# Where the transform matrices are made in the parameter stage, and what the first table round carries beside it

## The chip, the cores and the metric

The kernel runs on one core of a Trainium2 chip. The metric is the device time of one execution in microseconds (us); several executions of each kernel are timed and the median is taken. One more execution is recorded by the hardware profiler, and all durations below come from that one. Engines are named as in the profile: PE (matrix multiply), PEld (its weight loads), DVE (vector engine), ACT (scalar engine), POOL (GpSimd) and SP (the engine that issues most of the DMAs).

## What is computed

Two independent results are laid side by side. A is a recurrent attention block (2048 tokens in 64 segments of 32, a memory of 8 tokens carried from segment to segment). B is a long convolution whose 2048-tap filter is first built from complex parameters, then applied in the frequency domain. The change lies in front of both, in the stages that prepare B's filter and the part of A that does not depend on the carried memory.

```python
# B: filter, then convolution by FFT
dt = exp(log_dt)[:, None]
logdA = dt * (A_re + 1j * A_im);  dB = dt * (B_re + 1j * B_im)
P = exp(logdA[:, :, None] * l[None, None, :])          # D x N x L
K = einsum('dn,dnl,dn->dl', C_re + 1j * C_im, P, dB).real
y = irfft(rfft(pad(u)) * rfft(pad(K)))[:L] + u * Dskip
# A, for each segment s (mem is carried on):
h = concat([mem, x_s]);  q, k, v = h @ Wq, h @ Wk, h @ Wv
o = softmax(mask(q k^T * scale)) v @ Wo;  mem = o[:, :8];  out_s = o[:, 8:]
```

## The kernel before

`part_b` does B and, beside it, the projections of A for the 8 rows of every segment that never see the carried memory. Its first half has two stages that matter here.

**The parameter stage** (lines 679 to 856, inside one `with` block). Vector and scalar instructions turn the parameters into four tables x1 to x4 of 128 x 1024 numbers. Each is split by `put3` into three bf16 pieces (`hi`, `mid`, `lo`) that are stored to the DRAM tensor `PB`. Three other things are made meanwhile, as generators that `run` steps in turn:

- `modulus` and `angle`, which compute x4 and x3; x3 comes out last;
- `ahead.transposes` (lines 92 to 113): 16 blocks of x are loaded by POOL (`xb`), transposed by PE into `pt_x` (`ppt`, four PSUM banks) and copied by ACT into `xst` and `xTl`. The projections read the whole of `xTl`;
- `matrices` (lines 738 to 756): ten rounds that make the cosine and sine matrices `MF` of the transform. A full round is, on DVE, one absolute value (L744), one magic-number subtraction (L748) and two multiplies (L753), and on ACT a cosine (L745), a sine (L749) and a rounding (L755). Two rounds are made at the very start, three during the first `run`, the rest during the second.

An engine executes its instructions in the order in which they were written, so these pieces stand interleaved on DVE and ACT.

**The table stage** (loop over `f` from -1 to 16, lines 1159 to 1189). Sixteen rounds `r` of one table each go through the word list `ORDER`. A word with a prime belongs to round f-1, one without to round f. `X_t`, `X_p` are PE matmuls into `ptt` and `pa`; `k` (L1094) and `n` (L1100) reduce phases; `E` (L1088) takes exponentials on ACT; `S`, `C` take sines and cosines on ACT (L1105, L1114), with `b` (L1111) and `w` (L1118) on DVE between them; `gi`, `gr` (L1062, L1063) are the products on DVE; `K` (L949) and `x` (L957) form filter values, which are stored to `Kd`. E and S/C need different ACT tables, so each round has two ACT table loads (L1088, L1105).

The side jobs stand in the same list:

- `P0` to `P5` are six projection jobs. A job is one half of a weight slice: eight matmuls of 512 columns (L167) or sixteen of 256 (L154) into a PSUM tile of the pool `ps_k` (tag "s", four buffers), evicted later by a word `p0` to `p5` on DVE or ACT. There are 48 slices, so 96 jobs. The slice loads (`wsl`, L125, four buffers) are issued by SP three slices ahead. When the last job of a tensor is evicted, the stores of its results (`PKd`, or the eight row copies `VXd<-PVd`, L133) are put on a list `late`, from which each later eviction takes two.
- `U0` to `U3` are four jobs of `side` (L905): the forward transform of u with `MF`. They run in groups of four: results 0 and 1 are copied to `ua` on ACT, results 2 and 3 are subtracted and added on DVE into `us` (L916, L917), and after the fourth POOL combines them (`ux`, L921, L922, L924) and stores them to `Ud`. The first U job issues the loads `u_h` (L873) of u.
- `M` transposes one MF matrix (L884), evicted by `m` to `ms` and stored to `MId`.

Four P jobs are done before the loop. In the loop, side jobs run in every round from f = 0 on, primed words too; `evict_of` fixes which engine evicts. At f = 15 what is pending is flushed, `ahead.late` is emptied, and SP and POOL load the filter `KT` from `Kd` (L996). At f = 16 PE starts with `spectrum(0)` (L1050) and DVE with `negate` (KN, L1033). After the loop, the frequency-domain product (`pointwise`, L1224 to L1235 on DVE) begins.

Of the kernel before, what the change touches and what calls it, by code (L numbers as in the profile page):

```python
# [16 lines left out]
PSUM = bass.MemoryType.PSUM  # L17
# [628 lines left out]
def part_b(ctx, tc, u, A_re, A_im, B_re, B_im, C_re, C_im, log_dt, Dskip, out_b, ahead, copies, residents, first_state):  # L646
# [6 lines left out]
    v, sc, gp, pe, sy = nc.vector, nc.scalar, nc.gpsimd, nc.tensor, nc.sync  # L653
# [15 lines left out]
    MF = ahead.pool.tile([128, 4, 16, 2, 128], BF16, name="MF", tag="MF")  # L669

    ctx1 = ctx.enter_context(ExitStack())
    tabs = ctx1.enter_context(tc.tile_pool(name="b_tab", bufs=1))
    RE = tabs.tile([128, 8, NE], BF16, name="RE")
    RT = tabs.tile([128, 8, NT], BF16, name="RT")
# [5 lines left out]
    with tc.tile_pool(name="b_par", bufs=1) as par, tc.tile_pool(name="b_parh", bufs=2) as parh, tc.tile_pool(name="b_mg", bufs=2) as mg, \  # L680
# [11 lines left out]
        def f32(name):  # L692
            return par.tile(sh, F32, name=name)

        def put3(x, q, row):
            hi = parh.tile(sh, BF16, name="hi", tag="hi")
            sc.copy(out=hi[:], in_=x[:])
            sy.dma_start(out=PB[q][row].rearrange("t p n -> p t n"), in_=hi[:])
            yield
            v.tensor_tensor(out=x[:], in0=x[:], in1=hi[:], op=ALU.subtract)  # L700
            mid = parh.tile(sh, BF16, name="mid", tag="mid")
            sc.copy(out=mid[:], in_=x[:])
            sy.dma_start(out=PB[q][row + 1].rearrange("t p n -> p t n"), in_=mid[:])
            yield
            lo = parh.tile(sh, BF16, name="lo", tag="lo")
            v.tensor_tensor(out=lo[:], in0=x[:], in1=mid[:], op=ALU.subtract)
            sy.dma_start(out=PB[q][row + 2].rearrange("t p n -> p t n"), in_=lo[:])
            yield

        def run(*gens):  # L710
            gens = list(gens)
            while gens:
                for g in list(gens):
                    if next(g, g) is g:
                        gens.remove(g)
# [11 lines left out]
        def some(g, n):  # L727
            for _ in range(n):
                next(g, None)
                yield  # L730
# [7 lines left out]
        def matrices():  # L738

            tms, kMs = {}, {}  # L740
            for c in range(0, 20, 2):
                if 4 <= c:
                    tm = tms.pop(c - 4)
                    v.tensor_scalar(out=tm[:].bitcast(I32), in0=tm[:].bitcast(I32), scalar1=0x7FFFFFFF, scalar2=None, op0=ALU.bitwise_and)  # L744
                    sc.activation(out=sines(c - 4, 0), in_=columns(tm), func=ACT.Sin, scale=-TWO_PI, bias=hp[:])  # L745
                if 2 <= c < 18:
                    tm = tms[c - 2]
                    v.scalar_tensor_tensor(out=tm[:], in0=kMs.pop(c - 2)[:], scalar=MAGIC, in1=tm[:], op0=ALU.subtract, op1=ALU.subtract)  # L748
                    sc.activation(out=sines(c - 2, 1), in_=columns(tm), func=ACT.Sin, scale=-TWO_PI)  # L749
                if c < 16:  # L750
                    tms[c] = mg.tile([128, 2, 512], F32, name="tm", tag="tm", bufs=4)
                    for i in range(2):
                        v.tensor_scalar(out=tms[c][:, i], in0=colk[:], scalar1=rowl[:, c + i:c + i + 1], scalar2=None, op0=ALU.mult)  # L753
                    kMs[c] = mg.tile([128, 2, 512], F32, name="mkM", tag="mkM")
                    sc.activation(out=kMs[c][:], in_=tms[c][:], func=ACT.Identity, bias=magic[:])  # L755
                yield

        dt_b = dtb[:].unsqueeze(2).to_broadcast(sh)
        mats = matrices()
# [38 lines left out]
        x1, x2, x3, x4, x5, Wr, Wi = (f32(n_) for n_ in ("x1", "x2", "x3", "x4", "x5", "Wr", "Wi"))  # L798
# [14 lines left out]
        def modulus():  # L813

            sc.activation(out=y1[:], in_=Wi[:], func=ACT.Square)
            sc.activation(out=y2[:], in_=Wr[:], func=ACT.Square)
            yield
            v.tensor_tensor(out=x4[:], in0=y1[:], in1=y2[:], op=ALU.add)
            v.tensor_scalar(out=x4[:], in0=x4[:], scalar1=1.0e-37, scalar2=None, op0=ALU.max)
            sc.activation(out=x4[:], in_=x4[:], func=ACT.Ln)  # L820

            sc.activation(out=y1[:], in_=Wr[:], func=ACT.Abs)
            sc.activation(out=y2[:], in_=Wi[:], func=ACT.Abs)
            yield
            v.tensor_scalar(out=x4[:], in0=x4[:], scalar1=0.5, scalar2=None, op0=ALU.mult)
            yield

        def angle():

            v.tensor_tensor(out=x5[:], in0=y1[:], in1=y2[:], op=ALU.max)  # L830
            v.tensor_scalar(out=x5[:], in0=x5[:], scalar1=1.0e-37, scalar2=None, op0=ALU.max)
            v.reciprocal(out=x5[:], in_=x5[:])
            v.tensor_tensor(out=x3[:], in0=y1[:], in1=y2[:], op=ALU.min)
            v.tensor_tensor(out=x3[:], in0=x3[:], in1=x5[:], op=ALU.mult)
            sc.activation(out=x3[:], in_=x3[:], func=ACT.Arctan)
            yield
            v.tensor_scalar(out=x3[:], in0=x3[:], scalar1=float(1.0 / TWO_PI), scalar2=None, op0=ALU.mult)
            v.tensor_tensor(out=y1[:], in0=y2[:], in1=y1[:], op=ALU.is_gt)
            v.tensor_scalar(out=y2[:], in0=Wr[:], scalar1=0.0, scalar2=None, op0=ALU.is_lt)
            v.tensor_scalar(out=Wi[:], in0=Wi[:], scalar1=0.0, scalar2=None, op0=ALU.is_lt)  # L840
            yield
            for msk, top in ((y1, 0.25), (y2, 0.5)):
                v.tensor_scalar(out=x5[:], in0=x3[:], scalar1=-2.0, scalar2=top, op0=ALU.mult, op1=ALU.add)
                v.tensor_tensor(out=x5[:], in0=x5[:], in1=msk[:], op=ALU.mult)
                v.tensor_tensor(out=x3[:], in0=x3[:], in1=x5[:], op=ALU.add)
                yield
            v.tensor_scalar(out=Wi[:], in0=Wi[:], scalar1=-2.0, scalar2=1.0, op0=ALU.mult, op1=ALU.add)
            v.tensor_tensor(out=x3[:], in0=x3[:], in1=Wi[:], op=ALU.mult)
            yield
            yield from put3(x3, 1, 3)  # L850

        xs = ahead.transposes(prx, ppt, ident)
        pro = ahead.projections()
        next(pro)
        run(modulus(), put3(x2, 1, 0), put3(x1, 0, 0), some(xs, 9), some(mats, 3))
        run(xs, angle(), xs, put3(x4, 0, 3), xs, mats)


    tmp = ctx1.enter_context(tc.tile_pool(name="b_tmp", bufs=2))
# [2 lines left out]
    ctx_p = ctx.enter_context(ExitStack())  # L862
    ps_t = ctx_p.enter_context(tc.tile_pool(name="b_pst", bufs=2, space=PSUM))
    ps_e = ctx_p.enter_context(tc.tile_pool(name="b_pse", bufs=1, space=PSUM))
    ps_k = ctx1.enter_context(tc.tile_pool(name="b_psk", bufs=4, space=PSUM))

    u_r = u.rearrange("(c p r) d -> r p c d", p=128, r=4)

# [1 line left out]
    def load_uq(dq):  # L870
# [1 line left out]
        for r in range(4):  # L872
            sy.dma_start(out=t_[:, 4 * r:4 * r + 4, :], in_=u_r[r][:, :, DQ * dq:DQ * dq + DQ])  # L873
        return t_[:].rearrange("p c (t s e) -> p c s t e", t=4, e=8)

    def take(shape, dtype, name):
        return ps_k.tile(shape, dtype, name=name, tag="s")

    def matrices_back():
        for c in range(16):  # L880
# [269 lines left out]
    for eng, names in ((sc.copy, ON_ACT), (v.tensor_copy, ON_DVE)):  # L1150
        for nm, kind, slot in names:
            evict_of[nm] = (kind, slot, eng)
    evict = pro.send((take, tabs))
    for i in range(3):
        evict_next = next(pro)
        evict((sc.copy, v.tensor_copy)[i % 2])
        evict = evict_next
    evict(v.tensor_copy)
    for f in range(-1, 17):
        if f == 15:  # L1160
            for kind, slot in sorted(k for k in pending if k[0] == "P"):
                run_evict(kind, slot, v.tensor_copy)
            while ahead.late:
                ahead.late.pop(0)()
            ks = [load_k(0, DH, (sy, gp), ahead.pool.tile([128, 16, DH], BF16, name="KT", tag="kst"))]
        if f == 16:
            spectra = [load_u(0), load_u(1)]
        for word in ORDER:
            nm, r = word.rstrip("'"), f - word.endswith("'")
            if f == 16 and word == ORDER[0]:  # L1170
                s0 = ps_e.tile([128, 2, 512], F32, name="pa", tag="pa")
                s1 = [ps_t.tile([128, 512], F32, name="ptt", tag="ptt") for _ in range(2)]
                first = [[s0[:, half, :].rearrange("p (c d) -> p c d", c=2) for half in range(2)],
                         [t_[:].rearrange("p (c d) -> p c d", c=2) for t_ in s1]]
                negate(ks[0], v)
                spectrum(0, first)
            if nm in evict_of:
                run_evict(*evict_of[nm])
            elif nm[0] in side_ops:
                if f >= 0:  # L1180
                    run_side(nm[0], int(nm[1:] or 0))
            elif nm[0] == "X":
                e = int(nm[1])
                if 0 <= r <= 15 - (e == 0) or (r == -1 and e == 0):
                    table_ops[nm[2]](r, e)
            elif 0 <= r <= 15:
                table_ops[nm[:-1]](r, int(nm[-1]))
# [329 lines left out]
```

## Time and profile before

| | us |
|---|---|
| median of 3 runs | 2136.48 (2134.81 to 2144.58) |
| the profiled execution, device time | 2141.16 |
| the profiled execution, span of the trace | 2139.4 |

| busy over the span | share | instructions |
|---|---|---|
| PE | 88% | 33734 |
| DVE | 67% | 3353 |
| ACT | 49% | 1915 |
| POOL | 20% | 780 |

In the trace the parameter stage lies from 0 to about 83 us, the table stage from there to about 478 us, the frequency-domain part to about 728 us, and the attention segments behind it to the end. The page divides the span into 40 slices, so two slices cover the parameter stage and seven the table stage. A line of a timeline, as shown below, reads: start, duration, engine, source line, operation, output<-input with sizes, how many were merged, and in brackets how long the engine sat idle before it and what ended that. A line of stretches reads: the stretch, its length, and for each engine the busy time with the number of instructions, then the granted PE clock, the DMA share and GB/s.

### The profile page before, as it was taken

The page shows a single profiled execution, that of the slowest core. Times are in us where ns is not written, and L with a number is a line of the kernel's source. Part 1 is how long each engine was busy: PE and PEld are TensorE (multiplying, and loading weights), DVE is VectorE, ACT ScalarE, POOL GpSimd, SP SyncE. Part 2 cuts the span into 40 slices and gives each one's busy share as a digit, 9 for nine tenths or more (in the row PEclk, how much of TensorE's full clock was granted, in tenths as well). Part 3 has the DMA queues.
Part 4 walks back from the last instruction along what each step waited for, and adds up shares of the span by engine and source line. Part 5 has one row for each costly group of instructions (what it writes and reads, how often), then busy time and mean ns, then how long its engine had stood idle before and what let it go on. Part 6 is the DMA issues. An engine that isn't in the chain of part 4 may idle for free. (4 is left out here: it accounts for less than half of the span.)

```text
span 2139.4 us, 78633 instructions
## 1 busy us (share of the span) xinstructions
PE 1885.6 (88%) x33734; PEld 1183.7 (55%) x33734; DVE 1442.0 (67%) x3353; ACT 1045.2 (49%) x1915; POOL 435.8 (20%) x780
## 2 busy tenths in 40 slices
PE   1589999977999779999999999999998998999999
PEld 1365656656888535555555555555554555555554
DVE  8589999989999246566566665666655565666650
ACT  6699999971333324444444444444434343444430
POOL 2145445452111101111111111111111111111121
PEclk9999999989999889999999999999999999999999
DMA  6767886556745899999999999999998999999991
GB/s 162 191 198 229 241 226 176 163 174 204 242 134 175 302 350 328 324 324 338 319 337 333 325 322 324 328 335 338 324 321 302 320 323 317 308 334 334 327 335 57
DMA packets 344019, 590.78 MB, mean 276 GB/s; under 512 B 108537, under 2 KB 220185, under 8 KB 341621
## 3 DMA queue, kind: packets, MB, share of 16 engines
q1 hardware_dynamic: 297016, 528.00, 74.1%
q0 software_dynamic: 10544, 33.69, 4.6%
q10 hardware_dynamic: 36108, 24.07, 3.7%
q8 instruction: 264, 4.33, 0.8%
q14 instruction: 87, 0.70, 0.1%
HBM read 530.86 MB, written 65.26 MB: 279 GB/s over the span
## 5 line engine op out<-in xcount | busy, mean ns | idle before, releaser
L365 PEld LDWEIGHTS <-a_hT 128*32 128x32 bf16 x12352 | 337.5, 96 | 326.5 <-issue 79.6
L371 ACT CAST arena<-acc 128x512 bf16<-128x512 f32 x384 | 224.9, 586 | 421.2 <-PE acc L365 274.6
L365 PE MATMUL acc<-W,a_hT 128*32 128x512 bf16 x4864 | 376.1, 383 | 0.0
L474 PEld LDWEIGHTS <-arena 128*32 128x32 bf16 x8256 | 211.2, 97 | 110.8 <-issue 54.1
L365 PE MATMUL acc<-wst,a_hT 128*32 128x512 bf16 x2304 | 234.3, 385 | 40.2 <-DMA wst<-WD_v 28.9
L292 DVE TENSOR_SCALAR arena<-keep 128x256 int32<-128x256 int32 (+1 forms) x512 | 175.8, 395 | 35.6 <-PE acc L365 31.8
L379 POOL COPY arena<-arena 128x128 bf16<-128x128 bf16 x128 | 37.3, 292 | 720.9 <-PE tr L376 236.5
L474 PE MATMUL pp<-W_o,arena 128*32 128x256 bf16 x4608 | 171.9, 275 | 10.8 <-DMA W_o<-in_A_Wo_dram 6.7
L365 PE MATMUL acc<-MF,a_hT 128*32 128x512 bf16 x2048 | 158.7, 381 | 0.0
L414 DVE TENSOR_REDUCE a_mx<-sc 128x4 f32<-128x160 f32 (+1 forms) x192 | 73.0, 380 | 124.7 <-ACT sc L410 124.7
L167 PE MATMUL pro<-xTl,wsl 128*128 128x512 bf16 x512 | 119.8, 385 | 5.2 <-ACT xTl L111 5.2
L489 DVE COPY arena<-tr 128x512 bf16<-128x512 bf16 x64 | 27.2, 424 | 141.9 <-PE tr L376 96.7
L1050 PEld LDWEIGHTS <-MF 128*128 128x128 bf16 x1024 | 102.6, 101 | 29.9 <-issue 8.6
L410 ACT ACTIVATE sc<-sc 128x160 f32<-128x160 f32 (+1 forms) x192 | 64.2, 334 | 105.0 <-DVE sc L407 100.7
L437 POOL TENSOR_TENSOR arena<-arena,a_BD 128x128 bf16<-128x128 bf16 x128 | 68.5, 535 | 229.8 <-DVE arena L424 212.8
L460 ACT CAST arena<-pv 128x512 bf16<-128x512 f32 x128 | 75.1, 587 | 80.3 <-PE pp L444 59.0
L406 DVE TENSOR_REDUCE a_mx<-sc 128x4 f32<-128x160 f32 (+1 forms) x192 | 71.8, 374 | 59.2 <-PE sc L394 58.1
L567 ACT CAST arena<-pp 128x128 bf16<-128x128 f32 x128 | 27.8, 269 | 163.6 <-PE pp L474 163.6
L1050 PE MATMUL hps<-KT,MF 128*128 128x256 bf16 x720 | 94.1, 283 | 14.7 <-DVE x L1225 11.6
L1282 PE MATMUL yp<-Bt,MI 128*128 128x256 bf16 x680 | 102.8, 273 | 0.8 <-ACT yb L1298 0.8
L1088 ACT ACTIVATE E<-pa 128x648 bf16<-128x648 f32 x128 | 91.3, 713 | 17.9 <-PE pa L1080 14.2
L376 PEld LDWEIGHTS <-arena 128*128 128x128 bf16 x1024 | 57.9, 98 | 75.1 <-issue 37.4
(316 smaller groups left out, 4100.9 us busy)
## 6 DMA issues: line engine op xcount, KB each, us to landing
wst<-WD_v SPq DMA_DIRECT2D x256, 512.0 KB
wst<-WD_k SPq DMA_DIRECT2D x192, 512.0 KB
wst<-WD_o SPq DMA_DIRECT2D x192, 512.0 KB
wst<-WD_q SPq DMA_DIRECT2D x128, 512.0 KB
Ud<-ux POOLq DMA_DIRECT2D x16, 1024.0 KB, 6.0
uq<-Ud SPq DMA_DIRECT2D x32, 512.0 KB
wsl<-in_A_Wk_dram SPq DMA_DIRECT2D x16, 512.0 KB
wsl<-in_A_Wv_dram SPq DMA_DIRECT2D x16, 512.0 KB
```

The lines of the kernel that those rows point to most:

```text
L167: nc.tensor.matmul(a[:], lhsT=w[:, kc, 128 * j:128 * j + 128], rhs=xTl[:, kc, :, :].rearrange("p s k -> p (s k)"), start=(kc == 0), stop=( ...
L292: nc.vector.tensor_scalar(out=out.bitcast(I32), in0=in_.bitcast(I32), scalar1=0, scalar2=None, op0=ALU.bitwise_or)
L365: nc.tensor.matmul(a[32 * g:32 * g + 32, o_:o_ + rhs.shape[1]], lhsT=hT[:, kc, :], rhs=rhs, start=(kc == 0), stop=(kc == KC - 1), tile_pos ...
L371: nc.scalar.copy(out=q, in_=a[:])
L406: nc.vector.tensor_reduce(out=m_, in_=x, axis=AX.X, op=ALU.max)
L414: nc.vector.tensor_reduce(out=m_, in_=x, axis=AX.X, op=ALU.add)
L437: nc.gpsimd.tensor_tensor(out=L[:, 0].rearrange("p (a b) k -> p a b k", a=4), in0=bc(lt[:, :, 0:XL].unsqueeze(2), [128, 4, 4, XL]), in1=bc ...
L460: nc.scalar.copy(out=o, in_=p[:].rearrange("p a (g q) -> p a g q", g=4))
L474: nc.tensor.matmul(po[32 * qt:32 * qt + 32, o_:o_ + rhs.shape[1]], lhsT=oT[:, h % 4, (h % 16) // 4, :], rhs=rhs, start=False, stop=(h == 3 ...
L1050: pe.matmul(s_[r][half][:, cs, :], lhsT=MF[:, kc, 4 * rr + mc, cs, :], rhs=rhs, start=(i == 0 and mc == 0), stop=(i == 1 and mc == 3), ski ...
L1088: sc.activation(out=T["E", r, e // 4][:, lo:lo + 8 * NE].rearrange("p (i c) -> p i c", i=2), in_=T.pop(("p", r, e))[:, :, 0:4 * NE], func= ...
L1282: pe.matmul(yp[:, b, :], lhsT=m_[:, b, cs, kc, :], rhs=Bt[:, kc, j, half, c_, :], start=(kc == 0 and cs == 0 and half == 0), stop=(kc == 3 ...
```

## The change

`matrices` is taken out of both `run` calls. Its remaining eight rounds are now written behind the last parameter, in one loop with nine further P jobs: round, job, eviction of the job before, with ACT and DVE evicting in turn. So ten jobs instead of four are done before the table loop. For this the pool `ps_k` and `take` are opened before the parameter stage, at the other end of PSUM from `ppt`. In the table loop the side jobs of a word now also need r >= 0: at f = 0 the primed ones (P3, P4, P5, U2, U3, M) do not run. The generators hand out their jobs in sequence, so every later job moves forward or back accordingly; the evictions stay with their words.

```diff
     ctx1 = ctx.enter_context(ExitStack())
+    ps_k = ctx1.enter_context(tc.tile_pool(name="b_psk", bufs=4, space=PSUM, side="right"))
+
+    def take(shape, dtype, name):
+        return ps_k.tile(shape, dtype, name=name, tag="s")
...
         next(pro)
-        run(modulus(), put3(x2, 1, 0), put3(x1, 0, 0), some(xs, 9), some(mats, 3))
-        run(xs, angle(), xs, put3(x4, 0, 3), xs, mats)
+        run(modulus(), put3(x2, 1, 0), put3(x1, 0, 0), some(xs, 9))
+        run(xs, angle(), xs, put3(x4, 0, 3), xs)
+        evict = pro.send((take, tabs))
+        for i in range(9):
+            next(mats, None)
+            evict_next = next(pro)
+            evict((sc.copy, v.tensor_copy)[i % 2])
+            evict = evict_next
+        for _ in mats:
+            pass
+        evict(v.tensor_copy)
...
-    ps_k = ctx1.enter_context(tc.tile_pool(name="b_psk", bufs=4, space=PSUM))
...
-    evict = pro.send((take, tabs))
-    for i in range(3):
-        evict_next = next(pro)
-        evict((sc.copy, v.tensor_copy)[i % 2])
-        evict = evict_next
-    evict(v.tensor_copy)
     for f in range(-1, 17):
...
             elif nm[0] in side_ops:
-                if f >= 0:
+                if f >= 0 and r >= 0:
                     run_side(nm[0], int(nm[1:] or 0))
```

The list that orders the side jobs is this:

```python
ORDER = ("X0p' X0t' P3' b0' w0' C0' b1' P4' p3' C1' gi0' U2' P5' gr0' k0 n0 P0 E0 gr1' p4' X1t X1p p5' k1 X2t P1 E1 n1 p0 A1' k2 w1' X2p n2 "
         "X3t E2 U3' gi1' p1 X3p k3 X4t P2 E3 n3 k4 u1' X4p X5t p2 E4 U0 n4 k5 X5p n5 K0' E5 A0 X6p X6t E6 M' X7t k6 m' X7p U1 E7 x0' k7 K1' "
         "u0 K2' x1' S0 n6 K3' x2' n7 S1 x3'").split()
ON_ACT = (('p1', 'P', 1), ('p4', 'P', 4), ('A0', 'U', 0), ('A1', 'U', 2))
ON_DVE = (('p0', 'P', 0), ('p2', 'P', 2), ('p3', 'P', 3), ('p5', 'P', 5), ('u0', 'U', 1), ('u1', 'U', 3), ('m', 'M', 0))
```

More of the change, by code (lines that the diff above doesn't have):

```diff
@@ L874, in load_uq @@
         return t_[:].rearrange("p c (t s e) -> p c s t e", t=4, e=8)
-    def take(shape, dtype, name):
-        return ps_k.tile(shape, dtype, name=name, tag="s")
     def matrices_back():
```

## The prediction

> **What bounds it now.** The order of the views: first the busy time by stretches, to see which stage has idle engines; then the timelines of ACT, DVE and POOL in the table stage, to see what ends each wait. Parameter stage, first table round, and one of the later ones:
>
> ```profile
> 20.00:83.00 63.00, 12.03 (x96) 10.19 (x96) 54.80 (x59) 52.83 (x68) 6.04 (x11) 1.00 0.52 134
> 92.00:125.00 33.00, 27.93 (x160) 15.03 (x158) 19.08 (x27) 23.75 (x29) 10.50 (x12) 1.00 0.78 215
> 150.00:175.00 25.00, 23.29 (x282) 16.60 (x281) 23.62 (x38) 23.22 (x31) 10.50 (x12) 1.00 1.01 281
> ```
>
> From 20 to 83 us DVE (54.8 of 63) and ACT (52.8) bound; PE has nothing. In the first table round nobody is full. Later PE, DVE and ACT are all at 93 to 94%, so a round can be shortened only where one of them waits. The timeline gives the anchors:
>
> ```profile
> 80.16 1.22 DVE L706 TENSOR_TENSOR lo<-x,mid 128x1024 bf16<-128x1024 f32 x1 [1.11 <-ACT mid L702]
> 83.11 9.60 PE L167 MATMUL pro<-xTl,wsl 128*128 128x512 bf16 x32 [5.20 <-ACT xTl L111]
> 93.34 0.65 ACT L1094 ACTIVATE kM<-ptt,magic 128x464 f32<-128x464 f32 x1 [1.74 <-DMA wsl<-in_A_Wk_dram]
> 94.00 1.28 ACT L1088 ACT_TABLE_LOAD   x1
> ...
> 113.97 1.28 ACT L1105 ACT_TABLE_LOAD   x1
> ...
> 123.39 1.28 ACT L1088 ACT_TABLE_LOAD   x1
> ```
>
> The last piece ends at 81.4, projections start at 83.1 when ACT has made the last `xTl`, the first table begins on ACT at 93.3. From E load to E load the first round takes 29.39 us; the later loads stand at 123.39, 146.42, 169.45, 23.03 apart. The excess is in its E part (94.0 to 113.97, 20.0 against 13.57 later; the S part is 9.4 in both): P3', P4', U2', P5', P0 all stand on PE before X1, with no earlier round to cover them.
>
> **1. Matrices out of the parameter stage.** Struck from DVE: L744 eight times 0.69, L748 seven times 1.22, L753 twelve times 0.44, 19 us. Walking the remaining rows from 23.7: mid pieces of x1, x2 done 30.9, `reciprocal` ends 40.7, arctangent 43.3 to 44.3, x3 finished 57.9, hi, mid, lo of x3 to 62.5; the last `xTl` at 64.2, where ACT's 16 copies no longer stand behind cosines. So the projections start 18.9 us earlier. New small waits (lo for mid) eat what the vanished ACT waits give.
>
> **2. Matrices put back behind it.** ACT: a Sin table load (1.28) from 64.2; six rounds of cosine, sine, rounding, starting 1.05, 0.95 and 1.04 apart as at 60.11 to 63.15, 3.05 each, with some 0.3 us of waits for L748 in alternate rounds; one round of two, one of one; five evictions at 0.55. That is 1.3 + 18.3 + 0.9 + 2.1 + 1.1 + 2.7 = 26.4: ACT is free at 90.6. DVE needs under 3 us a round and hides. PE: ten jobs of 1.8 us (the first 3.4) lie inside, the tenth waits for the sixth eviction (about 85). The filter tables `pt` land by about 73. So the first kM moves from 93.3 to 90.6, **-2.7**, with six more jobs done.
>
> [...] The trace shows both sides: after 5 us idle at 442.8 the granted clock is 0.50 (448 to 452), after 1.6 us at 113.9 it stays 1.00. The new jobs are spaced by evictions, my largest gap is 2.9 us (80.0 to 82.9). [...]
>
> **3. First round.** Gone from it: three P (5.5 us of PE), two U (2.1), M (0.6). Its E part becomes that of a later round, 13.57, less 0.9 because U2' no longer delays E4 (PE's only wait there, 0.86). Against it: SP. Before, the loads `u_h` were issued at 94.0 and used at 98.1. Now two `wsl` loads stand in front, and the second needs the buffer that P1 frees, at about 95.9. Then 1.5 us to issue, 2.8 for four `u_h`, some 2 to land: 102.3, where U0 would stand at 99.0. PE waits 3.3 and E5 with it. E part 16.0, S part 8.8 (next step): 24.7 for 29.4, **-4.7** (bounds -7.5 if the loads land in time, -3).
>
> **4. POOL moves, which the diff does not say.** U jobs go in fours; dropping two at f = 0 shifts the fours by half a round. The fourth result, and POOL's 7.1 us of `ux`, move from u0 at the end of the E part to u1' in its middle. Now look at what DVE does beside them. POOL, then DVE, then ACT:
>
> ```profile
> 413.71 1.27 POOL L921 TENSOR_TENSOR ux<-us 128x512 f32<-128x512 f32 x1 [0.67 <-DVE us L916]
> 414.95 1.27 POOL L922 TENSOR_TENSOR ux<-us 128x512 f32<-128x512 f32 x1
> 416.18 4.67 POOL L924 TENSOR_TENSOR ux<-us 128x256 f32<-128x256 f32 x4
> ```
> ```profile
> 404.79 0.35 DVE L1118 TENSOR_SCALAR wn<-sn 128x768 bf16<-128x768 bf16 x1
> ...
> 416.30 1.59 DVE L1111 TENSOR_SCALAR nr<-nr 128x1856 int32<-128x1856 int32 x1
> 417.81 0.88 DVE L1118 TENSOR_SCALAR wn<-sn 128x768 bf16<-128x768 bf16 x1
> 418.61 1.65 DVE L1111 TENSOR_SCALAR nr<-nr 128x1856 int32<-128x1856 int32 x1
> ```
> ```profile
> 420.30 1.84 ACT L1114 ACTIVATE nr<-nr,hp 128x1856 bf16<-128x1856 f32 x1 [0.54 <-DVE nr L1111]
> ```
>
> The same `wn` takes 0.35 with POOL idle and 0.88 beside `ux`. L1111 is always beside `ux`; by L753 (0.43 for 512) and L744 (0.69 for 1024) it should take 1.11. In the changed order `us` is written at 407.7 of this frame, `ux` runs 408.4 to 415.6 and is over when L1111 starts at 416.3. There DVE does only work that reads PSUM (n, x, evictions), which keeps its 0.63, 0.42, 0.68 beside POOL already now (414 to 416, 420.2). So b, w, b end at 419.06, the wait of C1 goes and C1 starts when C0 ends, 419.67 instead of 420.30: 0.62 a round, all on ACT, with 1.26 us of PE wait before X1p to absorb it. Late next is C0 itself. Bounds 0 (E part fills it) and 1.3 (all of DVE's gain). Fourteen rounds from f = 1: **-8.7**. The granted PE clock plays no part.
>
> **5. The last rounds.** P2 leaves f = 14: E4's 0.86 wait goes, **-0.8**. At f = 15 two P jobs leave; before, PE idled there anyway: 0. DVE is unbroken from 462 to 474 (KN 1.74, b, w, b beside `ux`): by the same ratio **-2.1**.
> Added at f = 16: U2', U3' fall into PE's idle 467 to 474, 0; M' stands before K1' and is cold, **+0.9**; u1' and m' on DVE lie in waits for kp. Then `ux` (475 to 483) lies beside `pointwise`. [...] The nearest row, L1229 beside POOL's selects at 492.73, keeps 1.22, by it 0. I take **+0.5**.
> Moved on SP: v's last eviction is now at f = 14, so the eight `VXd<-PVd` (8.2 us of issue, about 11 us of full DMA, now at 486) come at 437, ahead of SP's 16 KT loads, for which KN and `spectrum(0)` wait (461.5, 459.7). POOL's 15 KT loads in turn start about 5 us earlier. KT before: last issue 455.7, used 460.3. After: SP issues until 457.3 and lands about 460 to 463. PE has 4 us to spare, DVE none: **+1.0** (0 to 5). Kd's last stores on POOL stand 7 us later behind `ux`, but SP reaches the loads that need them no earlier than now; nothing.
> From `pointwise` on everything is the same work, so the shift reaches the end.
>
> **Sum**: -2.7 - 4.7 - 8.7 - 0.8 - 2.1 + 0.9 + 0.5 + 1.0 = -16.6. The profiled execution, 2141.2, becomes 2124.6; it lies 4.7 above the median, so the median 2136.5 becomes **2120**.
>
> **Rivals.**
> *The POOL shift pays nothing*, because E's chain or PE takes the 0.62 back: without 8.7 and 2.1, -5.8, 2131. For it: PE at 93%. Against: its waits for E are longer than the gain. 0.22.
> *KT comes late* (the slower side): VXd's eight at the longest row of L133 (1.74) and SP's 16 KT loads at their longest (1.48) put the last issue at 474.7, and with 4.8 to land 479.5, 18.0 after DVE wants it; PE, idle so long, starts `spectrum(0)` cold, 1.7 more. -16.6 - 1.0 + 19.7 = +2.1, 2139; it decides against the change from 16 us of lateness. For it: 8192 packets of 256 B in front on one queue. Against: DMA was only 0.25 to 0.5 busy from 436 to 444. 0.08.
> *It hides more*: DVE's full 1.3 a round: 2110. 0.06.
> My own case 0.64, its own range 2115 to 2125.
>
> What a measurement tells from no change is about 0.5%, 10.7 us, the bound being 2125.8. Faster: nearly all of the first case and the third, 0.69; same, mainly the first rival, 0.25; slower 0.06. The range 2112 to 2132 leaves out the KT tail and the largest gain.
>
> **What will show it.** Last `lo` at 62, first pro matmul at 64, first kM near 90.6; E loads of rounds one and two 24 to 25 apart, later ones 22.4; L1111 at 1.1 and every L1118 at 0.35; C1 without a wait; a PE wait before the first `ups` for `u_h`; no DVE wait before KN above 1 us. I am wrong if L1111 stays at 1.6, if the rounds stay at 23.0 with L1111 short, or if KN starts late.

## The result, and the profile after

The changed kernel took 2116.93 us (median of 12 runs, 2109.57 to 2133.03) beside 2139.66 for the kernel before on the same chip (12 runs); the ratio is 0.9908 with a 95% interval of 0.9884 to 0.9933. A second comparison on one chip gave 2120.67 beside 2138.10, ratio 0.9925 (0.9898 to 0.9951). By these two ratios it is faster by 16 to 20 us; 2120 had been predicted, with a range of 2112 to 2132.

The profiled execution of the changed kernel happens to be the slowest of its 12 (2133.03 us, span 2131.3), only 8.1 us shorter in span than that of before. The stages explain this: up to the first copy of the attention part (ACT or DVE at L371) it is 15.2 us ahead (715.33 for 730.54), and in the attention part, which the change does not touch, it loses 7 again. In the thirteen profiles of this study that last part lasts 1391 to 1416 us, whatever the kernel. So single spans are not compared below; stages are. In the changed kernel most lines behind L669 stand a few further down than before, and in the variants again elsewhere; b is L1120, w L1127, `ux` L930 to L933.

Stretches of the changed kernel (columns as in the prediction's first view): the parameter stage, the first round, and a later one.

```profile
20.00:65.00 45.00, 11.56 (x96) 9.75 (x97) 38.12 (x34) 30.53 (x46) 6.97 (x11) 0.93 0.70 183
91.00:118.00 27.00, 20.65 (x112) 10.98 (x110) 14.41 (x22) 22.96 (x28) 2.16 (x4) 0.94 0.73 185
150.00:175.00 25.00, 24.01 (x311) 14.97 (x311) 21.90 (x37) 23.99 (x32) 11.41 (x17) 1.00 0.73 218
```

The parameter stage is 17 us shorter, by the start of the projections below. In the later stretch PE and ACT have risen to 96%, and DVE has fallen from 94 to 88%. The anchors of the table stage in the timelines:

```profile
62.94 1.23 DVE L710 TENSOR_TENSOR lo<-x,mid 128x1024 bf16<-128x1024 f32 x1 [2.69 <-ACT mid L706]
65.89 13.70 PE L167 MATMUL pro<-xTl,wsl 128*128 128x512 bf16 x56 [4.62 <-ACT xTl L111]
92.21 0.65 ACT L1103 ACTIVATE kM<-ptt,magic 128x464 f32<-128x464 f32 x1
92.88 1.28 ACT L1097 ACT_TABLE_LOAD   x1
...
108.44 1.28 ACT L1114 ACT_TABLE_LOAD   x1
...
117.14 1.28 ACT L1097 ACT_TABLE_LOAD   x1
```

Projections start at 65.9 (before 83.1), the first table at 92.2 (93.3), the first round takes 24.26 us (29.39). The later E loads are 22.1 apart (23.0). The groups of b, w, the cosine and the four small `ux`, over the whole run:

```profile
L1120 DVE TENSOR_SCALAR nr<-nr 128x1856 int32<-128x1856 int32 x32 | 36.1, 1127 | 4.7 <-ACT sn L1114 4.7
L1127 DVE TENSOR_SCALAR wn<-sn 128x768 bf16<-128x768 bf16 x32 | 11.3, 352 | 0.0
L1123 ACT ACTIVATE nr<-nr,hp 128x1856 bf16<-128x1856 f32 x32 | 57.0, 1827 | 0.6 <-DVE nr L1120 0.6
L933 POOL TENSOR_TENSOR ux<-us 128x256 f32<-128x256 f32 x64 | 44.5, 722 | 0.0
```

In the kernel before, the same groups had 51.8, 19.7 and 59.0 us busy and 74.8 on POOL, and ACT waited 10.2 us for b in front of the cosines (now 0.6). DVE's two operations and POOL's four are both shorter. That each had held up the other is tested below, by leaving `ux` out.

**What was given back.** The start of `pointwise` is 22.5 us earlier (456.10 for 478.62), but only 15.2 arrive at the attention part. First the kernel before, where `pointwise` starts at 478.62: GpSimd's last stores of `Kd`, SyncE's first loads for the second half of the filter, and ACT's wait for the last of those loads:

```profile
487.48 1.70 POOL L964 DMA_DIRECT2D Kd<-KxT  x3 [0.44 <-issue]
```
```profile
497.01 10.16 SPq L998 DMA_DIRECT2D KT<-Kd  x10
```
```profile
574.16 1.91 ACT L1036 ACTIVATE KN<-KT 128x2048 bf16<-128x2048 bf16 x1 [3.35 <-DMA W<-in_A_Wq_dram]
```

The changed kernel, GpSimd and SyncE around the start of `pointwise`, then ACT and PE 100 us later:

```profile
452.83 1.27 POOL L930 TENSOR_TENSOR ux<-us 128x512 f32<-128x512 f32 x1 [12.10 <-DVE us L925]
...
459.79 0.62 POOL L973 DMA_DIRECT2D Kd<-KxT  x1
463.13 2.95 POOL L973 DMA_DIRECT2D Kd<-KxT  x5 [2.73 <-issue]
466.58 1.28 POOL L973 DMA_DIRECT2D Kd<-KxT  x2 [0.50 <-issue]
470.82 0.58 POOL L973 DMA_DIRECT2D Kd<-KxT  x1 [2.95 <-issue]
...
479.34 1.71 POOL L973 DMA_DIRECT2D Kd<-KxT  x3 [1.95 <-issue]
```
```profile
466.12 0.83 SPq L1033 DMA_DIRECT2D uq<-Ud  x2
482.27 6.29 SPq L1007 DMA_DIRECT2D KT<-Kd  x10
```
```profile
557.03 1.91 ACT L1045 ACTIVATE KN<-KT 128x2048 bf16<-128x2048 bf16 x1 [9.01 <-DMA W<-in_A_Wq_dram]
```
```profile
560.97 0.40 PE L1285 MATMUL yp<-Bt,mn 128*128 128x256 bf16 x1 [4.91 <-ACT mn L1253]
```

GpSimd's last 18 stores of `Kd` now stand behind a `ux` and go out slowly, up to 481.0. SyncE is ready for the loads of the second half of the filter (`KT`, L1007) at 467.0 and waits until 482.3. These loads are paced, ten behind each `pointwise`, so they also end late, and ACT's `negate` (KN) waits 9.0 us for the last of them (before, 3.4). (The row names a load of `W`; a wait for several semaphores is put down to one of them, and which it was is shown below.) PE then waits for ACT's next copy. Steps 7 and 8 of `pointwise` (counted from 0) start 20.5 us apart instead of 14.0.

### The profile page after: what moved, and what is told of

It is laid out like the page before. It is cut to its first block, busy times and chain, and to the rows that moved or that the text cites. A ratio compares the mean times of both kernels' runs of the same rounds, so it can differ in the third digit from the quotient of the medians.

```text
span 2131.3 us, 78635 instructions
## 1 busy us (share of the span) xinstructions
PE 1889.4 (89%) x33734; PEld 1182.5 (55%) x33734; DVE 1415.6 (66%) x3352; ACT 1045.0 (49%) x1917; POOL 412.1 (19%) x780
## 5 line engine op out<-in xcount | busy, mean ns | idle before, releaser
L371 ACT CAST arena<-acc 128x512 bf16<-128x512 f32 x384 | 225.2, 586 | 432.4 <-PE acc L365 297.1
L489 DVE COPY arena<-tr 128x512 bf16<-128x512 bf16 x64 | 27.2, 425 | 149.3 <-PE tr L376 82.7
L1059 PEld LDWEIGHTS <-MF 128*128 128x128 bf16 x1024 | 101.9, 100 | 30.3 <-issue 10.2
L376 PE MATMUL tr<-a_ident,arena 128*128 128x128 bf16 x1024 | 83.0, 222 | 19.6 <-ACT arena L371 19.4
```

The source lines that it names most:

```text
L371: nc.scalar.copy(out=q, in_=a[:])
L376: nc.tensor.transpose(out=p[:, hl, :, :].rearrange("p a b -> p (a b)"), in_=q[:, 128 * hl:128 * hl + 128], identity=ident[:])
L1059: pe.matmul(s_[r][half][:, cs, :], lhsT=MF[:, kc, 4 * rr + mc, cs, :], rhs=rhs, start=(i == 0 and mc == 0), stop=(i == 1 and mc == 3), ski ...
```

## The experiments

All kernels in one table, in us from their profiles: the first kM, the first round, a later round (E load to E load), the start of `pointwise`, how long after that start the issue of the last pair of `KT` loads began, the time from it to the first copy of the attention part, and the place of that copy.

| kernel | kM | round 0 | later | pointwise | last KT | to L371 | L371 at |
|---|---|---|---|---|---|---|---|
| before | 93.3 | 29.4 | 23.0 | 478.6 | 89.5 | 251.9 | 730.5 |
| changed | 92.2 | 24.3 | 22.1 | 456.1 | 94.6 | 259.2 | 715.3 |
| changed_again | 90.6 | 23.1 | 22.1 | 454.2 | 92.7 | 255.8 | 710.0 |
| u_gate_alone | 93.5 | 26.5 | 22.1 | 459.7 | 98.2 | 262.0 | 721.7 |
| u_gate_off | 91.0 | 27.2 | 23.0 | 474.9 | 87.4 | 251.0 | 725.9 |
| gate_open | 90.7 | 27.3 | 23.0 | 473.4 | 86.7 | 250.5 | 723.9 |
| no_ux_before | 93.0 | 28.7 | 22.1 | 462.1 | 90.4 | 251.5 | 713.6 |
| no_ux_after | 91.9 | 25.0 | 22.1 | 457.2 | 90.4 | 251.5 | 708.7 |
| hold_pool | 90.7 | 25.0 | 22.1 | 456.1 | 96.0 | 260.6 | 716.7 |
| stores_on_sp | 90.6 | 25.2 | 22.1 | 456.1 | 92.5 | 254.4 | 710.5 |
| pe_filler | 90.6 | 23.4 | 22.1 | 453.9 | 94.9 | 259.2 | 713.1 |
| split_and_filler | 90.6 | 23.4 | 22.1 | 454.4 | 84.8 | 251.3 | 705.7 |
| split_only | 90.6 | 23.2 | 22.1 | 454.2 | 84.4 | 251.3 | 705.5 |

### Which part of the change shortens the rounds

The first kernel is the one before with the gate for the U jobs alone:

```diff
-                if f >= 0:
+                if f >= 0 and (r >= 0 or nm[0] != "U"):
```

> The kernel before with one edit: in round 0 the side job that belongs to round -1 is skipped for the U jobs only (P and M jobs and the parameter stage stay as before). Theory 'POOL moves' (the four ux operations no longer beside b, w, b of DVE): the later rounds take 22.1 us from E load to E load (before 23.03), L1111 falls to 1.13 us and L1118 to 0.35, rounds 1 to 14 give -13 us; the ux of the last round then stands ahead of the last Kd stores on POOL and about 7 us are given back behind pointwise: in all -5 to -9 us against before. Rival 'fewer projection jobs in the rounds' or 'the matrices behind': the rounds stay at 23.03 and the time at that of before.

2129.26 us, ratio 0.9953 (0.9924 to 0.9983). The rounds fall to 22.1 with the parameter stage and the P jobs as they were; at L371 it is 8.9 us ahead of before, with a give-back of 10.1 (262.0 for 251.9). The second is the changed kernel with the U jobs alone put back:

```diff
-                if f >= 0 and r >= 0:
+                if f >= 0 and (r >= 0 or nm[0] == "U"):
```

> The changed kernel with the U jobs alone put back to where they stood before (round -1 of U is issued in round 0; P and M jobs are still skipped there). Theory 'POOL moves': the later rounds go back to 23.0 us and b to 1.65 us, what stays is the start and the first round (-4 to -6 us), and the late Kd stores no longer stand behind a ux, so no wait of ACT for KT: 2133 to 2136 us beside 2139.7 before, so 15 us slower than the changed kernel up to pointwise and 9 to 12 at its end once the 7 us are not given back. Rival 'fewer projection jobs': the rounds stay at 22.1 us and the time near 2117.

2136.33 us, ratio 0.9991 (0.9968 to 1.0013). The rounds are back at 23.0, and b, w, b (here too L1120 and L1127) are long again:

```profile
411.79 1.58 DVE L1120 TENSOR_SCALAR nr<-nr 128x1856 int32<-128x1856 int32 x1
413.30 0.88 DVE L1127 TENSOR_SCALAR wn<-sn 128x768 bf16<-128x768 bf16 x1
414.10 1.65 DVE L1120 TENSOR_SCALAR nr<-nr 128x1856 int32<-128x1856 int32 x1
```

The give-back is gone as well (251.0). The third keeps the matrices behind the last parameter and the ten slices, and drops the gate (`if f >= 0:`).

> The changed kernel without the gate: round 0 issues all its side jobs, as before; the matrices behind the last parameter and the ten projection slices stay. Theory 'POOL moves': later rounds 23.0 us, b 1.65 us; E load at 92.9 as in the changed kernel, first round between 24.3 and 29.4; in all 0 to -4 us against before. Rival 'the move of the matrices is what pays': 2120 us or less.

2137.16 us, ratio 1.0011 (0.9986 to 1.0036); at L371 its profile is 6.7 us ahead of before, more than its runs confirm: the interval allows a gain of 3.0 us at most, and where the rest goes behind L371 is not known. So what the change is named for, the matrices and slices, gives 2.7 us at kM and 2.1 in the first round by the profile, and by the runs nothing that can be told from zero. Gating P and M as well changes nothing (round 0: 27.2 and 27.3).

### Is it GpSimd, or the place of the jobs?

Both kernels once more, with the six `ux` operations left out and the two `us` tiles stored instead, the same bytes:

```diff
-  x_ = up.tile([128, 4, 2, DQ], F32, name="ux", tag="ux")
-  gp.tensor_tensor(out=x_[:, 0], in0=e_[:, 0], in1=o_[:, 0], op=ALU.add)
...
-  gp.dma_start(out=Ud[kc, dq], in_=x_[:])
+  gp.dma_start(out=Ud[kc, dq][:, 0:2], in_=e_[:])
+  gp.dma_start(out=Ud[kc, dq][:, 2:4], in_=o_[:])
```

> The kernel before, with the six ux operations left out (the two us tiles are stored to Ud instead, the same bytes). Theory 'the ux operations on GpSimd beside b, w, b of DVE cost 0.95 us in each round': later rounds 22.1 us or a little less, L1111 1.13 us, L1118 0.35 us, with all jobs where they stood before. Rival 'the place of the U jobs on PE, ACT and DVE makes the round' : rounds stay at 23.03.

2126.62 us, ratio 0.9921 (0.9883 to 0.9960). All jobs of before stand where they stood, and the rounds are 22.1 (b and w are L1107 and L1114 here):

```profile
403.65 1.13 DVE L1107 TENSOR_SCALAR nr<-nr 128x1856 int32<-128x1856 int32 x1
404.69 0.35 DVE L1114 TENSOR_SCALAR wn<-sn 128x768 bf16<-128x768 bf16 x1
405.29 1.13 DVE L1107 TENSOR_SCALAR nr<-nr 128x1856 int32<-128x1856 int32 x1 [0.24 <-ACT sn L1101]
```

> The changed kernel with the six ux operations left out in the same way. If ux in its new place costs nothing more, the rounds stay at 22.08 us and the two kernels without ux have equal rounds; if a part of the cost was only moved to other operations of DVE, they fall by the rest, to 21.5 us or below.

2122.01 us, ratio 0.9909 (0.9869 to 0.9948), rounds 22.1. In its new place `ux` costs the rounds nothing that shows (22.08 us with it and without); the 0.95 us a round was its overlap with b, w, b. The rival, the place of the jobs, is out.

### Where the 7 us went

First attempt: round 16's `ux`, its `Ud` store and `MId` store are issued by GpSimd behind the last `Kd` stores instead of ahead (`rest` holds the six operations and the store).

```diff
+    held, hold = [], [False]
+    def later(g):
+        if hold[0]:
+            held.append(g)
+        else:
+            g()
...
-                gp.dma_start(out=MId[c], in_=ms[:])
+                later(lambda: gp.dma_start(out=MId[c], in_=ms[:]))
...
+                            later(rest)
...
+        hold[0] = f == 16
...
+    for g_ in held:
+        g_()
```

> The changed kernel with the GpSimd part of round 16's evictions (the six ux operations, the Ud store and the MId store) issued behind the last Kd stores instead of ahead of them; the DVE part stays in place. Theory 'the late Kd stores behind ux give back 7 us': the loads of KT for the second half start near 470 us instead of 482, ACT's negate waits no longer (9.0 us in the changed kernel), first attention eviction 6 to 7 us earlier: 2109 to 2111 us. Rival 'the give-back is contention of the loads themselves, or the stores wait for something else': no change (within 1 us of the changed kernel); or the held ux keeps its tile so long that what takes its place comes late: slower.

2121.41 us, ratio 0.9917 (0.9885 to 0.9949): no gain, and 260.6 from `pointwise` to L371. GpSimd's stores did end at 466.8, but the loads still started at 482.4. What SyncE waited for in 440 to 500 us (total, times, longest):

```profile
SPq L1017 <- DMA Ud<-ux: 9.0, 1, 9.0
SPq L1017 <- DMA Kd<-KxT: 5.8, 1, 5.8
```

One wait went and another took its place: the `KT` loads read `Kd`, not `Ud`, and yet wait for the `Ud` store, which now came last. So what they need from it must be memory. By the order in which the pools are closed and opened, the tile of `KT` lies where `ux` lay; no address in the record shows it. And `ux` now fell beside operations of `pointwise` that have all operands in SBUF:

```profile
465.70 3.45 DVE L1252 TENSOR_TENSOR Bt<-y 128x1024 bf16<-128x1024 f32 x2
469.08 1.21 DVE L1241 TENSOR_TENSOR x<-hps,osb__7315 128x1024 f32<-128x1024 f32 x1
...
472.76 1.63 DVE L1247 TENSOR_TENSOR x<-uq,x 128x1024 f32<-128x1024 f32 x1
474.32 1.74 DVE L1246 TENSOR_TENSOR y<-uq,x 128x1024 f32<-128x1024 f32 x1
```

`Bt` takes 2.36 to 2.38 and the products 1.22 when GpSimd computes nothing; `x`, which reads PSUM (`hps`), keeps its 1.21. Two steps of `pointwise` are longer by 1.1 us each.

Second attempt: `ux` stays early, and only the two stores go to SyncE, behind its own 18 `Kd` stores.

```diff
+    def store(out, in_):
+        if round_[0] < 16:
+            gp.dma_start(out=out, in_=in_)
+        else:
+            last.append(lambda: sy.dma_start(out=out, in_=in_))
...
+    for g_ in last:
+        g_()
```

> The changed kernel with the two stores of round 16's evictions (Ud 1 MB and MId 256 KB) issued by SyncE behind its last Kd stores instead of by GpSimd ahead of GpSimd's last Kd stores; the six ux operations stay where they are. The held variant showed that the tile of the KT loads lies where ux lay, so those loads wait for the Ud store too. Theory 'two waits, for the late Kd stores on GpSimd (with gaps of up to 3 us behind 1.25 MB of stores) and for Ud': GpSimd's Kd stores take 11 us without gaps and end near 470, Ud lands near 471, the loads of KT start at 471 to 473 (changed kernel 482.3), ACT's negate waits under 2 us (9.0), the first attention eviction comes 5 to 7 us earlier than in the changed kernel. Rival 'the loads of KT are slow in any place': start of the loads earlier, but negate's wait and the first eviction unchanged.

2117.46 us, ratio 0.9870 (0.9828 to 0.9911). Half a success: loads at 478.7, negate waits 6.7, 254.4 to L371. GpSimd's stores start at once and then stall again:

```profile
457.23 3.48 POOL L982 DMA_DIRECT2D Kd<-KxT  x6
461.26 1.82 POOL L982 DMA_DIRECT2D Kd<-KxT  x3 [0.55 <-issue]
...
469.73 0.59 POOL L982 DMA_DIRECT2D Kd<-KxT  x1 [3.04 <-issue]
...
475.02 1.08 POOL L982 DMA_DIRECT2D Kd<-KxT  x2 [2.46 <-issue]
```

Third attempt: SyncE takes 24 of the last 36 `Kd` stores and GpSimd 12, with the `Ud` store behind SyncE's 18th; once with the filler described below and once without.

```diff
-        f_((sy, gp)[n_ % 2])
+        f_((sy, gp, sy)[n_ % 3])
+        if n_ == 26:
+            last.pop(0)()
```

> The variant with the last two stores on SyncE, and in addition the filler matmuls in round 0 and the last 36 Kd stores shared 24 to SyncE and 12 to GpSimd (18 and 18 before), the Ud store behind SyncE's 18th. Theory 'what starts the KT loads is the last Kd store on GpSimd': GpSimd's stores end at 464 to 466 on the axis of the changed kernel, SyncE's at 468, the KT loads start at 469 to 473 (478.7 with 18 and 18), negate waits under 1 us (6.7), and pointwise steps 7 to 8 take 14.0 us instead of 18.4; with the filler's 1.6 us the first attention eviction comes at 704 to 706 us (715.3 in the changed kernel): 2108 to 2112 us. Rival 'the loads of KT or of uq, not their start, set negate's wait': start earlier, wait unchanged, first eviction near 709.

> The last variant without the filler matmuls. So far the first round took 24.3 to 25.2 us in four of five profiles with the gap of 2.4 us on TensorE (the next slice 2.75 to 3.12 us long) and 23.1 in the fifth (1.89), and 23.4 in both with the filler. Theory 'the gap makes the clock fall in most executions': first round 24.3 to 25.2 with the slice at 2.7 us or more, everything behind it as in the last variant (KT loads at 469 to 472, no wait of negate), first attention eviction 706 to 708 us, time 2110 to 2116. Rival 'the gap and the clock have no bearing on each other': 23.1 to 23.4 without the filler as well.

2111.63 us with the filler, ratio 0.9857 (0.9819 to 0.9895), and 2116.44 without, ratio 0.9887 (0.9858 to 0.9916); the intervals overlap and the two profiles are within 0.2 us of each other at L371. GpSimd's stores no longer stall, the loads start without a wait, and negate has none (GpSimd, SyncE and ACT, in the profile with the filler):

```profile
461.88 0.60 POOL L982 DMA_DIRECT2D Kd<-KxT  x1 [0.39 <-issue]
462.68 1.20 POOL L982 DMA_DIRECT2D Kd<-KxT  x2 [0.20 <-issue]
```
```profile
467.96 0.85 SPq L1042 DMA_DIRECT2D uq<-Ud  x2
469.70 6.95 SPq L1016 DMA_DIRECT2D KT<-Kd  x10
```
```profile
544.78 3.71 ACT L1054 ACTIVATE KN<-KT 128x2048 bf16<-128x2048 bf16 x2
```

The step from `pointwise` to L371 is back at 251.3. So the late `KT` loads are the give-back, and mending their start mends it. This is read from the stages: the interval of the ratio without the filler still overlaps that of the changed kernel. The table shows the price as a threshold: kernels whose last `KT` loads go out up to 90.4 us after `pointwise` begins need 250.5 to 251.9 us; from 92.5 us on they need 254.4 to 262.0. The kernel before stood at 89.5, so it had 1 to 3 us to spare.

### TensorE's clock in the first round

The skipped U jobs leave PE idle in round 0. In the changed kernel's profile, and in that of its repetition, the gap is the same and the slice behind it is not:

```profile
94.93 0.44 PE L1089 MATMUL pa<-RE,pt 128*128 128x324 bf16 x2 [2.40 <-ACT E L1097]
95.21 0.36 PE L1083 MATMUL ptt<-RT,pt 128*128 128x464 bf16 x1
95.41 3.06 PE L167 MATMUL pro<-xTl,wsl 128*128 128x512 bf16 x8
```
```profile
93.35 0.44 PE L1089 MATMUL pa<-RE,pt 128*128 128x324 bf16 x2 [2.40 <-ACT E L1097]
93.63 0.36 PE L1083 MATMUL ptt<-RT,pt 128*128 128x464 bf16 x1
93.82 1.89 PE L167 MATMUL pro<-xTl,wsl 128*128 128x512 bf16 x8
```

The granted clock from 94 to 98 us is 0.75 in the first and 1.00 in the second. A filler was put into the place of the skipped jobs:

```diff
                 if f >= 0 and r >= 0:
                     run_side(nm[0], int(nm[1:] or 0))
+                elif f == 0 and nm[0] == "U":
+                    fill = take([128, 2, DQ], F32, "fill")
+                    for i in range(8):
+                        pe.matmul(fill[:, i // 4, :], lhsT=MF[:, 0, i, 0, :], ...
```

> The changed kernel with eight matmuls of 256 columns on TensorE, read by nobody, in the places in round 0 of the U jobs that the gate skips. Theory 'the gap of 2.4 us that the skipped job leaves lowers the granted clock (0.75 in 94 to 98 us) and makes the next projection slice 2.8 to 3.1 us long instead of 1.9': the clock stays at 1.00 there, ACT's wait for pa before the third E falls from 2.4 to about 1.2 us, and the first round is 1 us shorter than 24.3 to 25.0. Rival 'the clock falls for another reason' : the clock stays at 0.6 to 0.75 and the first round at 24.3 to 25.0, or longer by the filler's own time.

2125.17 us, ratio 0.9919 (0.9888 to 0.9951); the clock is 1.00 there and the first round 23.4, and the same in the other kernel with the filler. But without it the first round is 23.1 and 23.2 in two profiles (changed_again, split_only) and 24.3 to 25.2 in four (changed, hold_pool, stores_on_sp, no_ux_after). So the low clock costs 1.1 to 2.0 us where it comes, it comes only in some executions after the same gap, and that the filler prevents it is not shown by two profiles.

Why only in some executions can be read from the clock in these profiles. In the table stage of the changed kernel the granted clock changes at 68.66, 85.72, 89.14, 95.96, 99.38, 423.64 and 433.88 us, in that of the kernel before at 446.67 and 453.49: within one profile all are whole multiples of 3.41 us apart, and from one profile to the other they are not. Here are two such stretches of the changed kernel, then two of its repetition:

```profile
92.55:95.96 3.41, 1.03 (x6) 0.58 (x6) 1.15 (x2) 3.38 (x5) 0.00 (x0) 1.00 0.12 36
95.96:99.38 3.42, 3.42 (x10) 1.18 (x8) 1.37 (x3) 1.04 (x3) 0.00 (x0) 0.50 0.00 0
```
```profile
88.83:92.24 3.41, 2.08 (x9) 0.87 (x9) 2.08 (x4) 3.12 (x4) 0.00 (x0) 1.00 0.42 127
92.24:95.65 3.41, 2.30 (x12) 1.17 (x12) 1.78 (x3) 2.82 (x5) 0.00 (x0) 1.00 0.00 0
```

In the first profile the whole gap lies in one stretch, of which PE is idle for 2.4 us, and the next stretch runs at half clock. In the second an edge divides the gap, so that the two stretches hold 1.3 and 1.1 us of idle time, and the clock stays at 1.00. In the other three profiles with a low clock (`hold_pool`, `stores_on_sp`, `no_ux_after`) the shares granted in 82 to 90 and 94 to 98 us (0.57 to 0.87) put the edges so that one stretch holds 2.3 to 2.4 us of the gap. `split_only` has 1.00 from 82 to 102 us, which shows no edge. Between 60 and 470 us the profiles of the kernel before and of the changed kernel together have 221 such stretches at full clock; PE's idle time in them follows from the modelled ends of its matmuls. Five have 2.28 to 3.41 us of idle time, and half clock followed each of them; the other 216 have at most 1.65, and it followed none. So the gap of 2.40 us was followed by half clock in the four profiles where it lay in one stretch, and not in the one where an edge is seen to divide it. With the filler the gap is 1.5 us, less than any idle time that half clock followed in those two profiles; that is an argument, not a test.

> The changed kernel once more, on the same chip: its stages up to the first attention eviction at 713 to 716 us, its time 2115 to 2122 us; what lies behind that eviction varies from one execution to the next by some 10 us in the six profiles so far (1396 to 1416 us), whatever the kernel, and is to do so here.

Its time and ratio are given at the start. At L371 it stands at 710.0, 3 us earlier than expected: round 0 had the full clock, and its `KT` loads started at 477.0, so that 4 us were given back, not 7. The attention part took 1400.2 us.

## Why the prediction was right, step by step

The time and direction were right, and so was the main mechanism, GpSimd beside DVE. That the sum came so near is in part luck: the rounds and the stretch behind them gave 6.6 us more than predicted, and 7.3 us that had been put at nothing were given back.

- **Start (-2.7).** In eight of ten profiles with the moved matrices the first kM stands at 90.6 to 91.0, as worked out. In the changed kernel's own profile it was -1.1: ACT waited 1.9 us for a buffer `xst` whose store had not ended, which delayed the middle piece of x3 and all behind it.
- **First round (-4.7).** -5.1, and -6.2 in the repetition. About 2.1 come from the matrices and slices (gate_open) and about 2.9 from the skipped U jobs (u_gate_alone). The wait for `u_h` was priced at 3.3 us and was 0.7 to 1.3. The term holds nothing for PE's clock behind the 2.40 us gap; it stayed at 1.00 in two of six profiles without filler and was 0.57 to 0.75 over 4 us in four. The gap among the ten jobs that the prediction put at 2.9 us (2.0 to 2.8, near 83 us) was followed by a lower clock in six of ten profiles (0.61 to 0.78 over 4 us); the first kM did not suffer (90.6 in three of them).
- **POOL moves (-8.7).** The mechanism, which the diff does not state, is confirmed by both kernels without `ux`. The term was mis-sized: 0.95 a round instead of 0.62, in fourteen rounds -13.2. The prediction counted ACT's wait before C1 and no more. ACT's cosines gain 0.66 a round (4.13 to 3.47 us from the start of C0 to the instruction behind the two), C0 itself starts 0.12 earlier, and the wait of E4 falls from 0.86 to 0.69 in every round.
- **P2 out of f = 14 (-0.8).** -0.4: that round is 21.7 us long instead of 22.1. E4's wait went, but E5 then waited 0.37.
- **Last rounds (-2.1, +0.9, +1.0 for KT).** Together -0.2 was expected from the last E load to `pointwise`; it was -2.7, and -2.0 in the repetition. With `ux` left out of the kernel before it was -2.2, near the first of the three terms; of the two costs nothing shows in these sums. KN starts without a wait (442.27 us), so the rival "KT comes late" did not come true at that place.
- **`ux` beside `pointwise` (+0.5).** No run shows the 0.5 that stands in the sum. In the changed kernel it was nothing: `ux` ends at 458.1, when DVE is still at operations that read PSUM (1.23 and 1.21 us). The held variant shows what the other case costs, 2.2 us.
- **The step that failed.** "Kd's last stores on POOL stand 7 us later behind `ux`, but SP reaches the loads that need them no earlier than now; nothing". It was 7.3 us, 3.9 in the repetition. SP does reach the loads earlier: 10.9 us after `pointwise` begins, instead of 18.4. The prediction itself had moved the eight `VXd<-PVd` away from that place on SP and did not draw the consequence. And the stores are not 7 us later but 14 (they end 24.9 us after the start of `pointwise`, before 10.6), because 18 of them take 21 us behind the `Ud` store; before, the last 15 took 11 us there. The loads had 1 to 3 us of cover, which was not looked up.

The sum of the steps up to L371 in the changed kernel's profile: -1.1 - 5.1 - 13.2 - 0.4 - 2.7 + 7.3 = -15.2, inside the interval of the ratio (-24.8 to -14.3 us of 2139.7).

What stays open: why GpSimd's stores stall for 2 to 5 us in some versions. They do around 1 MB transfers (`Ud`, `uq`) and not where the small stores are out before these. DVE's work alone is not the reason: in the first 10 us of `pointwise` its operations are the same in the kernel before, where the gaps between the stores are 0.4 to 0.65 us, and in the changed kernel, where one is 2.7. How the transfers would do it was not tested. And why the attention part varies by up to 25 us.

## What to carry to other kernels

A change of counts in one generator moves work of another engine in phase: look at what each engine does at the same moment before and after, because two engines can lengthen each other's operations while neither waits; here DVE's b took 1.65 us beside GpSimd's `ux` and 1.13 apart from it. When a step is "nothing" because something else covers it, look up how long the cover is; here it was 1 to 3 us out of 90. When one wait is removed and the time stays, ask what else the waiting load needs: its memory, not only its data.

## What the hardware showed that was not expected

- GpSimd's f32 additions and DVE's one-operand operations cost each other: b 1.13 to 1.65 us, w 0.35 to 0.88, and the four small `ux` 722 ns each instead of 1195 once they are apart. The DVE operations that read PSUM were not lengthened in these profiles (n keeps 0.63 beside `ux`, x of `pointwise` 1.21).
- With the small stores shared 18 to 18, GpSimd's were out at 476.1 us and SyncE's at 463.9 (`stores_on_sp`); shared 24 to 12, with `Ud` moved as well, the last went out at 467.0.
- The same 2.40 us gap on TensorE is followed by full clock in two executions and by 0.57 to 0.75 over 4 us in four. Between the changed kernel's profile and its repetition it differs in how it lies to the 3.41 us stretches at whose edges the clock changed.
